# Attention, then two expert layers: the V products and row sums of a pair of heads gathered into three stretches

## The chip, the cores and the metric

The kernel runs on one core of a Trainium2 chip. The metric is the device time of one execution in microseconds (us). The kernel before has three timed runs; one further execution was recorded by the hardware profiler, and every row shown here is from that one.

## The reference, cut to what matters

```python
def _attn_ref(q, k, v, f):            # batch 4, heads 8, S = 576, D = 64
    scores = scale * np.matmul(q, k.transpose(0, 1, 3, 2))
    cum = np.cumsum(np.log(np.clip(f, 0.0001, 1.0)), axis=-1)
    scores = np.where(causal, -1e9, scores + cum[:, :, :, None] - cum[:, :, None, :])
    attn = np.exp(scores - np.max(scores, axis=-1, keepdims=True))
    attn = attn / (np.sum(attn, axis=-1, keepdims=True) + 1e-09)
    return np.matmul(attn, v)
...
x = attn_out as 2304 tokens x 512
h = x @ w_in; x = (h * sigmoid(h)) @ w_out      # 512 -> 2048 -> 512
x = soft mixture of 8 experts over x (phi, w1, w2)
```

The weights `w_in` and `w_out` arrive as 64-bit numbers, two 32-bit words each, and the kernel turns them into single precision itself. The change is to the attention alone; the two layers behind it stay as they are.

## The kernel before, in words

**Pairs and half steps.** The 32 heads are worked in 16 pairs. The loop runs over half steps `i`; `p, h = divmod(i, 2)` gives the pair and the half. `att_step(i, cv)` reads its half of the string `ORDER` (the two halves are divided by `|`) and issues one small piece of work for each word. The engines' queues are in program order, so this string is the order in which TensorE, VectorE (DVE), ScalarE (ACT), GpSimd (POOL) and the DMA queue on SyncE (SP) see their work. Several stages are in flight at a time: in the two half steps of pair `p` the kernel computes the scores of pair `p`, the products with V and the row sums of pair `p-1`, the row maxima one and a half pairs ahead, and it prepares Q and K of pair `p+2` and loads pair `p+3`.

**The words.**
- `s0` to `s5` (`s_piece`): two score matmuls into one of three banks, then the exponential on ACT (L232), then on POOL the causal select (L234).
- `m0` to `m5` (`max_piece`): one matmul (L178) into one of three other banks and a masked maximum on DVE (L184). The last block has two column ranges: `m4` reduces the first into `Mx` (L181), `m5` the second into a column of `Mt`.
- `f0`, `f1` (`max_fin_a`, `max_fin_b`): the maximum of those two columns (L197); then a transpose on TensorE, a copy to `mr` on DVE (L206), and a DMA of the maxima into row 127 of `QA`, which the score matmuls read.
- `v0` to `v3` (`av`): seven pieces of the products with V a pair (L269). The operands are plain single precision, so each piece is four matmuls (two heads, two passes); a head fills 64 columns of the array. `r` (`row_sums`): 44 matmuls of 32 columns (L252), a copy `RS` on ACT (L255), a DMA `sg<-RS`.
- `n` (`norm_b`): reciprocals of the sums on DVE (L284, L285), a DMA `R<-sg` to memory, and four DMAs `RB<-R` that read it back spread over the partitions. `b` (`norm_c`): three DVE multiplications by `RB` (L305).
- `q0`, `q1` (`split_hi`): two ACT copies each that round Q (`QA`, `QB`) and K (`KA`, `KB`). `z0`, `z1` (`split_lo`): their remainders on POOL (L154, L156).
- `l0` (`load`): one DMA of 1152 KB with Q and K of a pair, into two buffers in turn. `w`: V of a pair. `p` (`spread`): two small rows of `KA`.
- `c`: a phase of the conversion of a raw weight block. Eight blocks are converted in the attention, beginning at the half steps `CONV_AT`, in four phases each; at the end of the last, `release()` lets `pump()` issue the next raw load of 512 KB.

The 24 further raw blocks are converted in the first part of the dense layer, which starts when the attention's buffers are given back.

Of the kernel before, what the change touches and what calls it, by code (L numbers as in the profile page):

```python
# [9 lines left out]
F32 = mybir.dt.float32  # L10
F32R = mybir.dt.float32r
# [6 lines left out]
ORDER = "v0 m0 q0 v1 v2 m1 m2 s0 s1 f0 m3 z0 p s2 a3 s3 m4 r s4 l0 s5 c m5 z1 f1 | q1 v0 v1 s0 l1 f0 f1 s1 s2 z0 b n v2 m0 m1 v3 m2 w s3 m3 s4 z1 m4 s5 m5 a3 c"  # L18
CONV_AT = (2, 6, 10, 14, 18, 22, 28, 29)
# [14 lines left out]
def tile_attention_moe_softmoe(ctx: ExitStack, tc: tile.TileContext, qk, vr, f, wcat, phi, w1, w2, out):  # L34
# [35 lines left out]
    fc = ld.tile([NH, 2, S], F32, name="fc", tag="qk", bufs=2)  # L70
# [50 lines left out]
    def load(p):  # L121
# [7 lines left out]
        t = ld.tile([128, 2, 2, S], F32, name="qk", tag="qk", bufs=2)  # L129
        staged[p] = t[:, 0], t[:, 1]  # L130
        nc.sync.dma_start(out=t, in_=src)
# [6 lines left out]
    def split_hi(p, which):  # L138
        src = staged[p][which]
        nm, keep_in = (("QB", QB), ("KB", KB))[which]  # L140
        t = keep_in[p] = att.tile([128, 2, S], F32R, name=nm, tag=nm, bufs=3)
        if which:
            nc.scalar.activation(KA[p % 3][0:64], src[0:64], AF.Copy)
            nc.scalar.activation(t[64:128], src[64:128], AF.Copy)
        else:
            nc.scalar.activation(QA[p % 3][0:64, :, 64:640], src[0:64], AF.Copy)
            nc.scalar.activation(t, src, AF.Copy)  # L147
# [21 lines left out]
    def max_piece(i, j):  # L169
# [12 lines left out]
        else:  # L182
            junk = att.tile([128, 448], BF16, name="junk", tag="junk", bufs=2)
            nc.vector.tensor_tensor_reduce(out=junk[:, 0:w], in0=t[:, 0:w], in1=mask[:, 448 - w:448], scale=1.0,  # L184
                                           scalar=-3e38, op0=ALU.add, op1=ALU.max,
# [4 lines left out]
    MAXED, FIN = set(), []  # L190

    def max_fin_a():
        if not FIN and fins and 2 * fins[0][0] + fins[0][1] + fins[0][2] - 1 in MAXED:
            FIN.append(fins.pop(0))
            p, h0, n = FIN[0]
            last = Mt[p][:, h0:h0 + n, 4:5]
            nc.vector.tensor_tensor(last, last, Mx[p][:, h0:h0 + n], ALU.max)  # L197

    def max_fin_b():
        if not FIN:  # L200
            return
        p, h0, n = FIN.pop()
# [35 lines left out]
    SUMS, READY, done = set(), set(), {"r": 0, "n": 0, "b": 0}  # L238
# [43 lines left out]
    def norm_b(p):  # L282
# [4 lines left out]
        nc.sync.dma_start(out=r, in_=sg)  # L287
        if p < NPAIR - 1:
# [18 lines left out]
    def att_step(i, cv):  # L307
# [7 lines left out]
        def cvt(n, ph):  # L315
            if ph == 0:
                conv_b(n)
                conv_c(n)
            elif ph == 1:
                conv_d(n, 0)  # L320
                conv_d(n, 1)
            elif ph == 2:
# [7 lines left out]
        for op in ORDER.split("|")[h].split():  # L330
# [12 lines left out]
            elif k == "q" and 0 <= p + 2 < NPAIR:  # L343
                split_hi(p + 2, h)
# [12 lines left out]
            elif k == "c":  # L357
                for n, ph in cv:
                    cvt(n, ph)
# [691 lines left out]
```

## Time and profile before

| | us |
|---|---|
| median of three runs | 590.6 |
| lowest, highest | 589.3, 594.24 |
| profiled execution, its own time | 591.06 |
| its span in the trace | 589.2 |
| TensorE busy | 542.8 (92%) |
| ACT, DVE, POOL busy | 327.5, 320.7, 214.0 |

The span runs from the first to the last instruction; the execution's own time is 1.9 us longer. Busy TensorE is counted from modelled ends of pipelined matmuls, so a stretch can be full and still have slack in it. Attention fills roughly the first 215 us.

### The profile page before, as it was taken

The page shows a single profiled execution, that of the slowest core. Times are in us where ns is not written, and L with a number is a line of the kernel's source. Part 1 is how long each engine was busy: PE and PEld are TensorE (multiplying, and loading weights), DVE is VectorE, ACT ScalarE, POOL GpSimd, SP SyncE. Part 2 cuts the span into 40 slices and gives each one's busy share as a digit, 9 for nine tenths or more (in the row PEclk, how much of TensorE's full clock was granted, in tenths as well). Part 3 has the DMA queues.
Part 4 walks back from the last instruction along what each step waited for, and adds up shares of the span by engine and source line. Part 5 has one row for each costly group of instructions (what it writes and reads, how often), then busy time and mean ns, then how long its engine had stood idle before and what let it go on. Part 6 is the DMA issues. An engine that isn't in the chain of part 4 may idle for free.

```text
span 589.2 us, 11255 instructions
## 1 busy us (share of the span) xinstructions
PE 542.8 (92%) x4151; PEld 377.2 (64%) x4151; DVE 320.7 (54%) x889; ACT 327.5 (56%) x686; POOL 214.0 (36%) x294
## 2 busy tenths in 40 slices
PE   3589999999999999899999999999989999969993
PEld 2466666666666777677777777667666667624542
DVE  7557667677575569999989422422522431321113
ACT  5588878887877576467646544433433423322022
POOL 6378777787767421656465200000000000002000
PEclk9999999999999999999999999999999999988997
DMA  5655555646552267702431501121332228499978
GB/s 208 195 180 161 173 179 165 216 132 194 172 171 74 64 181 300 267 36 72 143 108 72 215 0 37 44 101 36 108 144 71 95 73 305 163 350 348 348 243 256
DMA packets 49528, 94.32 MB, mean 160 GB/s; under 512 B 7330, under 2 KB 34754, under 8 KB 47554
## 3 DMA queue, kind: packets, MB, share of 16 engines
q1 hardware_dynamic: 49474, 93.61, 48.3%
q8 instruction: 32, 0.52, 0.4%
q14 instruction: 22, 0.18, 0.1%
HBM read 83.64 MB, written 9.13 MB: 157 GB/s over the span
## 4 chain that ended last, share of the span: by engine, by line
PE 75%; DVE 9%; ACT 6%; DMA 5%; issue 3%; POOL 1%; SPq 0%; ACTq 0%; DVEq 0%; POOLq 0%
PE h L539 9%; PE h L541 9%; PE h L540 9%; PE av L269 7%; PE gtp L571 6%; PE mx L178 5%; PE rs L252 5%; PE st L227 5%; PE st L229 3%; PE lp L580 3%; PE pp L689 3%; DMA qk<-in_qk_dram 3%; PE so L818 3%; PE h L752 2%; DVE wt L445 2%
## 5 line engine op out<-in xcount | busy, mean ns | idle before, releaser
L539 PE MATMUL h<-w,xh 128*128 128x512 f32 x288 | 117.0, 406 | 2.6 <-DVE gt L561 2.5
L541 PE MATMUL h<-w,xh 128*128 128x512 f32 x288 | 113.6, 394 | 0.0
L540 PE MATMUL h<-w,xl 128*128 128x512 f32 x288 | 113.4, 394 | 0.0
L561 DVE SCALAR_TENSOR_TENSOR gt<-gt,h 128x512 f32<-128x512 f32 (+1 forms) x73 | 48.5, 675 | 104.8 <-ACT gt L554 104.7
L554 ACT ACTIVATE gt<-h 128x512 f32<-128x512 f32 (+1 forms) x73 | 42.8, 590 | 88.8 <-PE h L541 83.1
L184 DVE CUSTOM_DVE_ANT_0 junk<-mx,mask 128x64 bf16<-128x64 f32 (+4 forms) x160 | 65.9, 428 | 35.0 <-PE mx L178 32.2
L178 PE MATMUL mx<-KA,QA 127*128 127x256 f32 (+2 forms) x192 | 64.0, 378 | 15.7 <-POOL QB L156 9.3
L234 POOL TENSOR_SCALAR_AFFINE_SELECT E<-E 128x128 f32<-128x128 f32 (+1 forms) x160 | 52.0, 338 | 54.2 <-ACT E L232 53.0
L727 POOL MEMSET SM<- 128x512 f32 x2 | 1.1, 526 | 192.6 <-ACT gt L554 190.2
L232 ACT ACTIVATE E<-st 128x256 f32<-128x256 f32 (+2 forms) x192 | 63.4, 389 | 10.7 <-PE st L229 9.4
L227 PE MATMUL st<-QA,KA 128*128 128x256 f32 (+1 forms) x192 | 60.9, 328 | 4.3 <-ACT E L232 4.0
L539 PEld LDWEIGHTS h<-w,xh 128*128 128x128 f32 x288 | 54.1, 188 | 16.4 <-DVE gt L561 4.4
L541 PEld LDWEIGHTS h<-w,xh 128*128 128x128 f32 x288 | 54.1, 188 | 12.8
L540 PEld LDWEIGHTS h<-w,xl 128*128 128x128 f32 x288 | 54.2, 188 | 11.2
L269 PE MATMUL av<-E,VF 128*64 128x320 f32 (+4 forms) x448 | 60.0, 373 | 0.0
L178 PEld LDWEIGHTS mx<-KA,QA 127*128 127x128 f32 x192 | 36.1, 202 | 35.5 <-POOL QB L156 9.3
L229 PE MATMUL st<-QB,KB 128*128 128x256 f32 (+1 forms) x192 | 54.6, 299 | 0.0
L572 ACT ACTIVATE gr<-gtp 128x512 f32<-128x512 f32 x72 | 38.9, 593 | 18.4 <-PE gtp L571 18.4
L227 PEld LDWEIGHTS st<-QA,KA 128*128 128x128 f32 x192 | 35.4, 185 | 18.9 <-ACT E L232 8.8
L156 POOL TENSOR_TENSOR QB<-qk,QB 64x576 fp32r<-64x576 f32 x30 | 42.9, 1431 | 7.3 <-ACT QB L147 5.0
L571 PE MATMUL gtp<-ident,gt 128*128 128x128 f32 x288 | 40.2, 282 | 3.9 <-ACT gr L572 2.3
L571 PEld LDWEIGHTS gtp<-ident,gt 128*128 128x128 f32 x288 | 30.7, 141 | 17.1 <-issue 6.7
(145 smaller groups left out, 853.4 us busy)
## 6 DMA issues: line engine op xcount, KB each, us to landing
unit<-in_w_dram SPq DMA_DIRECT2D x64, 512.0 KB
qk<-in_qk_dram SPq DMA_DIRECT2D x15, 1152.0 KB
raw<-in_w_dram SPq DMA_DIRECT2D x32, 512.0 KB
VF<-in_v_dram SPq DMA_DIRECT2D x16, 320.0 KB
RB<-R SPq DMA_DIRECT2D x64, 72.0 KB
WO<-wt SPq DMA_DIRECT2D x8, 512.0 KB
unit<-WO SPq DMA_DIRECT2D x8, 512.0 KB
out_dram<-ob SPq DMA_DIRECT2D x16, 256.0 KB
```

The costliest lines, as they stand in the source:

```text
L178: nc.tensor.matmul(t[:, 0:n], lhsT=qa[0:127, h, 128 * blk:128 * blk + 128], rhs=ka[0:127, h, k0:k0 + n], start=True, stop=True)
L184: nc.vector.tensor_tensor_reduce(out=junk[:, 0:w], in0=t[:, 0:w], in1=mask[:, 448 - w:448], scale=1.0, scalar=-3e38, op0=ALU.add, op1=ALU.max,
L227: nc.tensor.matmul(t[0:m, 0:n], lhsT=ka[:, h, k0:k0 + m], rhs=qa[:, h, 64 + q0:64 + q1], start=True, stop=False)
L229: nc.tensor.matmul(t[0:m, 0:n], lhsT=kb_[:, h, k0:k0 + m], rhs=qb[:, h, q0:q1], start=False, stop=True)
L232: nc.scalar.activation(e[0:m, c0:c0 + n - skip], t[0:m, skip:n], AF.Exp, scale=0.125)
L234: nc.gpsimd.affine_select(out=e[0:m, 0:m], in_=e[0:m, 0:m], pattern=[[1, m]], compare_op=ALU.is_ge, fill=0.0, base=0, channel_multiplier=-1)
L269: nc.tensor.matmul(AVP[p][x][64 * h:64 * h + 64, o0:o0 + n], lhsT=VF[p % 2][0:k, kb, h], rhs=E[2 * p + h][kb][0:k, c:c + n], start=kb == 0 ...
L539: nc.tensor.matmul(o, lhsT=xh[:, d, tok], rhs=w[:, 0], start=(d == 0), stop=False)
L540: nc.tensor.matmul(o, lhsT=xl[:, d, tok], rhs=w[:, 0], start=False, stop=False)
L541: nc.tensor.matmul(o, lhsT=xh[:, d, tok], rhs=w[:, 1], start=False, stop=(d == 3))
L561: nc.vector.scalar_tensor_tensor(g, g, 1.0, h[:, n * j:n * j + n], op0=ALU.add, op1=ALU.mult)
L571: nc.tensor.transpose(tp[:, j, 128 * t:128 * t + 128], g[:, t, 128 * u:128 * u + 128], ident)
```

## The change

`ORDER` is written anew. The products with V of a pair stand in two places, `v0 v1 v2 v3` at the start of the first half step (pieces 0 to 3) and `v1 v2 v3` in the middle of the second (pieces 4 to 6); with the row sums `r` that makes three stretches. Score pieces and maximum pieces alternate. The remaining words follow:

- `max_fin_a` and L197 go. The maximum of `m5` begins from `Mx` (a pointer operand in place of the constant), and one `f` does the rest, behind the second stretch of V products.
- `split_hi` is four words of one ACT copy each: `q1` (KA), `q0` (QA), `q3` (KB), `q2` (QB). `split_lo` names matrix and head; the remainder of Q's second head is made half a step later (`z01`).
- Q and K of a pair are two DMAs of 576 KB into buffers of their own, `l1` (K) and `l0` (Q).
- `norm_b` ends with `R<-sg`; the four `RB<-R` become a word of their own, `x` (`norm_x`), in the next half step. `n` moves to the end of the second half step.
- Conversion phases 0 to 4 in place of 0 to 3; `CONV_AT` ends in 26, 28. The raw loads of the attention are no longer issued from the end of a conversion, but by a new word `g`, which stands just ahead of `n`.
- `spread` runs one pair earlier, at the end of the second half step.

```diff
-ORDER = "v0 m0 q0 v1 v2 m1 m2 s0 s1 f0 m3 z0 p s2 a3 s3 m4 r s4 l0 s5 c m5 z1 f1 | q1 v0 v1 s0 l1 f0 f1 s1 s2 z0 b n v2 m0 m1 v3 m2 w s3 m3 s4 z1 m4 s5 m5 a3 c"
-CONV_AT = (2, 6, 10, 14, 18, 22, 28, 29)
+ORDER = "q1 v0 v1 v2 v3 s0 m0 s1 m1 a3 s2 m2 x z01 l1 s3 m3 q0 c r l0 s4 m4 s5 m5 | s0 m0 s1 m1 s2 m2 q3 v1 v2 v3 b f q2 s3 z10 m3 s4 m4 z11 s5 m5 w p z00 f g n c"
+CONV_AT = (2, 6, 10, 14, 18, 22, 26, 28)
...
-        t = ld.tile([128, 2, 2, S], F32, name="qk", tag="qk", bufs=2)
-        staged[p] = t[:, 0], t[:, 1]
-        nc.sync.dma_start(out=t, in_=src)
+        for c in cs:
+            t = ld.tile([128, 2, S], F32, name="qk"[c], tag="qk"[c], bufs=2)
+            staged.setdefault(p, [None, None])[c] = t
+            nc.sync.dma_start(out=t, in_=src[:, c])
...
+    def split_hi(p, j):
+        src = staged[p][j % 2]
+        if j == 0:
+            nc.scalar.activation(QA[p % 3][0:64, :, 64:640], src[0:64], AF.Copy)
+        elif j == 1:
             nc.scalar.activation(KA[p % 3][0:64], src[0:64], AF.Copy)
+        elif j == 2:
+            QB[p] = att.tile([128, 2, S], F32R, name="QB", tag="QB", bufs=3)
+            nc.scalar.activation(QB[p], src, AF.Copy)
+        else:
+            KB[p] = att.tile([128, 2, S], F32R, name="KB", tag="KB", bufs=3)
+            nc.scalar.activation(KB[p][64:128], src[64:128], AF.Copy)
...
-                                           scalar=-3e38, op0=ALU.add, op1=ALU.max,
+                                           scalar=Mx[p][:, h] if j == 5 else -3e38, op0=ALU.add, op1=ALU.max,
...
-            last = Mt[p][:, h0:h0 + n, 4:5]
-            nc.vector.tensor_tensor(last, last, Mx[p][:, h0:h0 + n], ALU.max)
...
         nc.sync.dma_start(out=r, in_=sg)
+        RT[p] = r
+
+    def norm_x(p):
+        r = RT[p]
...
             if ph == 0:
                 conv_b(n)
+            elif ph == 1:
                 conv_c(n)
-            elif ph == 1:
+            elif ph == 2:
...
+            elif k == "x" and done["x"] < done["n"]:
+                norm_x(done["x"])
+                done["x"] += 1
...
+            elif k == "g":
+                pump()
...
-        release(*(x for x in (sl,) if x))
+        if sl:
+            release(sl)
...
-            cv = [(n, i - b) for n, b in enumerate(CONV_AT) if 0 <= i - b < 4]
+            cv = [(n, i - b) for n, b in enumerate(CONV_AT) if 0 <= i - b < 5]
```

## Rows read from the trace of the kernel before

**Rows 1.** Busy time by stretch: length, PE, PEld, DVE, ACT, POOL, clock, DMA.
```profile
109.43:121.35 11.92, 11.71 (x110) 8.00 (x110) 8.43 (x32) 9.66 (x21) 9.09 (x15) 1.00 0.66 196
121.35:133.19 11.84, 11.71 (x110) 8.00 (x109) 8.12 (x31) 10.34 (x22) 9.56 (x16) 1.00 0.50 156
...
215.00:300.00 85.00, 82.21 (x407) 64.36 (x404) 82.79 (x144) 51.21 (x99) 41.79 (x29) 1.00 0.44 160
```

**Rows 2.** TensorE in order of time (start, length): row sums, first and thirteenth.
```profile
37.93 1.31 PE L252 MATMUL rs<-E,ones 128*32 128x288 f32 x30
...
183.28 1.78 PE L252 MATMUL rs<-E,ones 128*32 128x288 f32 x44
```

**Rows 3.** Chain of waits, one piece of it.
```profile
100.53 5.45 DMA qk<-in_qk_dram
```

**Rows 4.** TensorE in order of time, around the V products of one pair.
```profile
111.88 1.30 PE L269 MATMUL av<-E,VF 128*64 128x320 f32 x8
113.11 0.39 PE L227 MATMUL st<-QA,KA 128*128 128x256 f32 x1
113.33 0.28 PE L229 MATMUL st<-QB,KB 128*128 128x256 f32 x1
113.45 0.27 PE L204 MATMUL mtp<-ident,Mt 128*10 128x128 f32 x1
...
116.72 0.38 PE L178 MATMUL mx<-KA,QA 127*128 127x288 f32 x1
117.03 0.65 PE L269 MATMUL av<-E,VF 128*64 128x256 f32 x4
117.61 0.39 PE L178 MATMUL mx<-KA,QA 127*128 127x256 f32 x1
117.93 0.98 PE L269 MATMUL av<-E,VF 128*64 128x128 f32 x8
118.84 0.53 PE L178 MATMUL mx<-KA,QA 127*128 127x256 f32 x2
```

**Rows 5.** TensorE where the maxima have ended and V pieces stand together.
```profile
208.63 0.81 PE L269 MATMUL av<-E,VF 128*64 128x192 f32 x8
209.37 0.41 PE L227 MATMUL st<-QA,KA 128*128 128x320 f32 x1
...
210.19 1.41 PE L269 MATMUL av<-E,VF 128*64 128x256 f32 x12
211.53 1.78 PE L252 MATMUL rs<-E,ones 128*32 128x288 f32 x44
```

**Rows 6.** DMA issues on SyncE in order of time: start, length.
```profile
98.38 0.53 SPq L136 DMA_DIRECT2D VF<-in_v_dram  x1
99.02 0.27 SPq L164 DMA_DIRECT2D KA<-cumd  x1
...
114.07 0.80 SPq L207 DMA_DIRECT2D QA<-mr  x1
115.23 0.35 SPq L287 DMA_DIRECT2D R<-sg  x1
118.28 0.66 SPq L295 DMA_DIRECT2D RB<-R  x1
...
200.60 0.34 SPq L287 DMA_DIRECT2D R<-sg  x1
202.11 0.66 SPq L295 DMA_DIRECT2D RB<-R  x1
...
207.06 0.45 SPq L417 DMA_DIRECT2D raw<-in_w_dram  x1
...
211.43 0.62 SPq L295 DMA_DIRECT2D RB<-R  x1
```

**Rows 7.** VectorE in order of time: copy of the maxima, multiplications by RB.
```profile
113.76 0.28 DVE L206 CAST mr<-mtp 10x128 fp32r<-10x128 f32 x1 [1.11 <-PE mtp L204]
...
207.35 0.90 DVE L305 TENSOR_TENSOR x<-UB,RB 128x256 f32<-128x256 f32 x3 [2.92 <-DMA RB<-R]
```

More of the change, by code (lines that the diff above doesn't have):

```diff
@@ L67, in tile_attention_moe_softmoe @@
     warm = keep.tile([1, 1], F32, name="warm")
-    fc = ld.tile([NH, 2, S], F32, name="fc", tag="qk", bufs=2)
+    fc = ld.tile([NH, 2, S], F32, name="fc", tag="q", bufs=2)
     ft, c8 = fc[:, 0], fc[:, 1]
@@ L119, in tile_attention_moe_softmoe, with load @@
     QB, KB = {}, {}
-    def load(p):
+    def load(p, cs=(0, 1)):
         b, hp = divmod(p, NP)
@@ L188, in max_piece, with max_fin @@
             MAXED.add(i)
[L190 to L195, printed above, removed]
-            last = Mt[p][:, h0:h0 + n, 4:5]
-            nc.vector.tensor_tensor(last, last, Mx[p][:, h0:h0 + n], ALU.max)
-    def max_fin_b():
-        if not FIN:
+    MAXED = set()
+    def max_fin():
+        if not (fins and 2 * fins[0][0] + fins[0][1] + fins[0][2] - 1 in MAXED):
             return
-        p, h0, n = FIN.pop()
+        p, h0, n = fins.pop(0)
         tp = bank(RING_T, [5 * n, 128], "mtp")
@@ L237, in tile_attention_moe_softmoe @@
     AVP, U, RT = {}, {}, {}
-    SUMS, READY, done = set(), set(), {"r": 0, "n": 0, "b": 0}
+    SUMS, READY, done = set(), set(), {"r": 0, "n": 0, "x": 0, "b": 0}
     CUT = 144
@@ L317, in cvt @@
                 conv_b(n)
+            elif ph == 1:
                 conv_c(n)
-            elif ph == 1:
+            elif ph == 2:
                 conv_d(n, 0)
                 conv_d(n, 1)
-            elif ph == 2:
+            elif ph == 3:
                 conv_d(n, 2)
@@ L343, in att_step @@
             elif k == "q" and 0 <= p + 2 < NPAIR:
-                split_hi(p + 2, h)
-            elif k == "z" and 0 <= p + 2 < NPAIR:
-                split_lo(p + 2, h, int(j))
+                split_hi(p + 2, int(j))
+            elif k == "z" and 0 <= (i + 3) // 2 < NPAIR:
+                split_lo((i + 3) // 2, int(j[0]), int(j[1]))
             elif k == "f":
-                (max_fin_b if j == "1" else max_fin_a)()
+                max_fin()
             elif k == "n" and done["n"] < min(done["r"], NPAIR - 1):
@@ L351, in att_step @@
                 done["n"] += 1
-            elif k == "b" and done["b"] < done["n"] and done["b"] in READY:
+            elif k == "b" and done["b"] < done["x"] and done["b"] in READY:
                 norm_c(done["b"])
                 done["b"] += 1
-            elif k == "p" and h == 0 and 0 < p + 2 < NPAIR:
-                spread(p + 2)
+            elif k == "p" and 0 < p + 3 < NPAIR:
+                spread(p + 3)
+            elif k == "x" and done["x"] < done["n"]:
+                norm_x(done["x"])
+                done["x"] += 1
             elif k == "c":
@@ L359, in att_step @@
                     cvt(n, ph)
+            elif k == "g":
+                pump()
             elif k == "w" and 0 <= p + 1 < NPAIR:
                 load_v(p + 1)
-            elif k == "l" and h == 0 and 3 <= p + 3 < NPAIR:
-                load(p + 3)
+            elif k == "l" and 3 <= p + 3 < NPAIR:
+                load(p + 3, (int(j),))
     FREE, units = [], []
@@ L912, in tile_attention_moe_softmoe @@
             norm_b(p)
+        for p in range(done["x"], NPAIR - 1):
+            norm_x(p)
         for p in range(done["b"], NPAIR - 1):
@@ L992, in tile_attention_moe_softmoe @@
                 norm_b(NPAIR - 1)
+                norm_x(NPAIR - 1)
             if k == 3:
```

8 lines of the change are left out of this document (removed).

## Prediction

> **What bounds the kernel now.** I read the busy time by stretch first. Behind the attention DVE is busy for 82.79 of 85 us in the third row [rows 1], with conversions that cannot begin before the attention gives its buffers back. So whatever the attention's end moves, the end of the kernel moves too, one to one, and only the attention is costed here. Its pace is read off the row sums, of which there is one stretch a pair: from the first to the thirteenth it is (183.28 - 37.93) / 12 = 12.11 us a pair [rows 2]; two ordinary pairs take 11.92 and 11.84, with TensorE busy for 11.71 of each [rows 1]. That looks like TensorE and nothing else, but the chain of waits tells of a second bound of the same length: it runs through the load of Q and K, 5.45 us [rows 3]. This load stands in SP's queue behind the copy `sg<-RS`, so behind this pair's row sums, and the two copies of the next pair's `q0` wait for it, with the exponentials and the next row sums behind them: a loop that closes once a pair. A faster TensorE alone would run into it.
>
> The TensorE rows show why a full engine still has something to give. The granted clock is 1.00 there [rows 1], and between full-width matmuls the next start comes after about 2.4 columns a nanosecond: 0.12 us for 256 columns (113.33 to 113.45 [rows 4]). Around a stretch of V products it does not. The matmul ahead, 288 columns, takes 0.31 (116.72 to 117.03); the first one behind, 256 columns, takes 0.22 in place of 0.12 (113.11 to 113.33); one between two stretches takes 0.32 (117.61 to 117.93). The stretch has a cost of its own too: its columns pass at 1.2 a nanosecond, twice, and on top come 0.15 to 0.16: a lone piece of 256 columns takes 0.58 (2 x 0.213 + 0.15), pieces 3 and 4 together 1.23 (4 x 0.267 + 0.16) [rows 4].
>
> **Part 1, three stretches for six.** Before, a pair has five stretches of V products: 0.58, 0.91, 1.23 [rows 4], and the last two pieces 0.74 as they stand together in one row [rows 5]; 3.46 in all. After: pieces 0 to 2 together take 1.34 (210.19 to 211.53 [rows 5]), against 0.58 + 0.91 = 1.49 apart, so merging takes off 0.15; piece 3 adds 2 x 0.267 = 0.53: 1.87. Pieces 4 to 6: 0.53 + 0.74 = 1.27. Sum 3.14, gain 0.32. Pieces 5 and 6 differ in the rows of the array that they fill (128 and 64); that they stand apart before costs no less than the 0.74, so this can only understate the gain. Three first-matmuls-behind fewer: 3 x 0.10 = 0.30. Entries: 0.18 ahead of two of the five (0.31 less 0.13 for 288 columns), about 0.1 ahead of the others; 0.66 becomes 0.18 + 0.10, gain 0.38. Together 1.0 us a pair, and TensorE's own pace 11.71 - 1.0 = 10.7, or 10.6, since some of the 11.71 is itself the tail of a wait.
>
> The row shows that 64-column and full-width work do not follow each other freely, at about 0.35 a stretch. The Trainium skill ("TensorEngine Tiling (Array Packing)", Tiling Modes) has the rule: a change of tiling mode drains the engine. By it the 128-to-64-row step inside the second stretch stays, as the 0.74 has it; without it the second stretch would be 1.12, and the sum 2 us better over the attention.
>
> **Part 2, two loads for one.** The same bytes, one more issue of about 0.45 on SP (as the raw load's issue [rows 6]); behind it waits `sg<-RS`, which waits for the row sums anyway. K is now needed first and is issued ahead of `sg<-RS`; Q is needed only at `q0`, half a pair later than before. The loop of [rows 3] opens by several us: I take it as gone. With it go the two pairs of some 13 us that the mean of 12.11 has over the ordinary 11.9.
>
> **Part 3, the round trip of the sums: the new loop.** Before, `n` issued `R` early in a second half step, the four `RB` DMAs followed, and `b` used them a whole pair later. Now `n` is at the end of the second half step, `x` follows in SP's queue, and `b` stands in the middle of the next second half step, on DVE ahead of the copy `mr` and of the maxima `m3` to `m5`. The matmul of `m5` needs the bank that `mr` empties (three banks in turn), and the next pair's first V stretch is queued behind it. So: `mr`, then `R`, then `RB`, then `b`, then the next `mr` is a loop that closes once a pair. Its length: from `mr` to the issue of `R` it was 1.47 (113.76 [rows 7] to 115.23 [rows 6]), with `QA<-mr` in between; now V (0.64 from issue to issue, 98.38 to 99.02) and the rows of KA (0.27) are issued there also, and DVE needs the three maxima first: I take 2.1. From `R` to the first `RB`: 1.51 with nothing in flight (200.60 to 202.11), 3.05 behind a load of 1152 KB (115.23 to 118.28) [rows 6]; now V's 320 KB is ahead, so 2.3, in the middle. First `RB` to the multiplications: 5.24 (202.11 [rows 6] to 207.35 [rows 7]). Three multiplications to `mr`: 0.83 (0.90 less overlap). Sum 10.5, about TensorE's 10.6, so nothing is left over.
>
> In five of these twelve pairs the word `g` puts a raw load of 512 KB just ahead of `R`. The nearest row: a raw load issued at 207.06, the first `RB` at 211.43, 4.37 later [rows 6]. With its issue, 0.45, the loop becomes 2.1 + 4.8 + 5.2 + 0.4 = 12.5 (the first term without the part that the raw load now covers would be 12.0 at the least). A pair of 12.5 is not made good by the next, whose own loop is 10.5. Before, the raw loads went out early in a second half step, where nothing of that pair waited for them.
>
> **Part 4, at nothing.** L197 goes, two columns wide and off TensorE's path. The pointer operand of `m5` is in no row: 0 to 0.2 us an instruction (the small DVE operations nearby), and it lies in the loop once a pair; I take 0 and keep 2 us in the range. The four ACT copies are the same; `q1` now lies under the first V stretch, `q0` under the row sums, `q3` under the second stretch, where ACT has no scores to work on. Without that cover each would hold up a score bank for 1.1 us. POOL's remainders are needed a pair later and keep that slack. Five conversion phases have the same instructions; DVE's in the first half step now lie under the row sums. `spread` makes SP wait for the pair's last score matmul, with raw load and `R` behind it; the 0.27 is counted. Start-up: the same loads with two more issues, -1 to +1, taken as 0.
>
> **The sum**, against the profiled execution's 591.06. Twelve intervals before: 145.35. After: 7 x 10.6 + 5 x 12.5 = 136.7, less 0.8 for the time that `m5` can wait in the first late pair: 135.9, a gain of 9.4. The thirteenth interval gains 1.0, the first pair and the last two one stretch each, 0.3 to 0.4: together 1.1. 591.06 - 11.5 = 579.5; I say **579**. The median before lies 0.5 under the profiled run, within its spread.
>
> **Rivals.** *The loop has slack* (if `R` lands within 1.5 us, and the raw load passes it or is covered): TensorE's 10.6 holds in all twelve: 127.2, gain 18.1 + 2.1: 571. For it: 1.51 is seen, and V is small. Against it: `R` has waited behind whatever was queued in every other row.
>
> *ACT becomes the bound.* It is busy for 10.0 a pair (mean of 9.66 and 10.34 [rows 1]); at 10.6 it would be 94% full, and in an in-order queue that meets banks of three, not all of its idle time of 1.9 can go. If 1.6 of it stays, the pace is 11.6: 145.4 - 139.2 = 6.2 and 1 at the ends: 584. The Trainium skill ("Perfetto Trace Analysis", Identifying the Most-Contended Engine) speaks for it: matmul busy time is no measure of how near TensorE is to its limit, LDWEIGHTS busy is, while for ACT occupancy is. By that TensorE is at 8.0 of 11.92 and ACT at 84% the engine to relieve, and this change relieves it of nothing.
>
> *Slower: the sums' round trip runs behind the half loads.* If K or Q is still in flight when `R` is issued, because `sg<-RS` holds Q back, `R` waits for up to half of 5.45 more. The loop is then 13.2, and 15.2 with a raw load: 7 x 13.2 + 5 x 15.2 = 168.4, 23 us more, 612. It decides from a mean loop of 12.11, which is reached when `R` to `RB` takes 0.8 us more than my mean.
>
> *The change does not do what it says:* stretches merge but the cost sits in the weights of each piece, and the new order gives it back in waits; 587 to 592.
>
> **How the numbers follow.** A run of this kernel can tell about 1% from no change, 5.9 us. Chances: the forecast 0.43 (574 to 584), the loop with slack 0.25 (567 to 574), ACT 0.13 (581 to 588), no gain 0.11, slower by the round trip 0.08. Faster by over 1% (under 585): nearly all of the first two and over half of the third, 0.75. Slower by over 1%: 0.08. Within 1%: 0.17. The range leaves out the upper tail of the last two and a little below: 567 to 590.
>
> **What would show it.** The V products in two stretches a pair of about 1.87 and 1.27; row sums 10.6 apart, and some 12 apart where a raw load lies ahead of `R`; no ACT wait for Q and K in the ordinary pairs; DVE idle ahead of its multiplications by `RB`, and TensorE at the last maximum of a pair waiting for DVE. Wrong if ACT shows no idle time and TensorE waits for exponentials, if `RB` has landed well before its use, or if the layer behind the attention does not move with it.

## The result and the profile after

The changed kernel takes 597.0 us (median of four runs), the kernel before 590.9 on the same chip: a ratio of 1.013, 95% interval 1.008 to 1.017. It is slower by 1.3% where I had forecast 2% faster. The profiled execution took 599.4 us, with a span of 597.7; it is 2.4 us slower than the median, and the rows below are read from it.

First the row sums on TensorE (start, length), which answer to [rows 2], and the first matmul of the layer behind the attention.

```profile
40.50 1.31 PE L248 MATMUL rs<-E,ones 128*32 128x288 f32 x29
...
189.27 1.78 PE L248 MATMUL rs<-E,ones 128*32 128x288 f32 x44
...
223.12 0.50 PE L546 MATMUL h<-w,xh 128*128 128x512 f32 x1
```

The first row sums come 2.6 us later than before, the twelve intervals take 148.8 us instead of 145.4 (a mean of 12.40 instead of 12.11), and from the thirteenth row sums to the first `h` matmul it is 33.9 instead of 31.8 (before, that matmul stood at 215.05). Together 8.1 us, and the whole span is longer by 8.5: what the attention loses, the end loses.

The busy time of two neighbouring pairs, from row sums to row sums, in the columns of [rows 1]; the second one waits for an `RB` whose `R` stood behind a raw load.

```profile
88.58:99.46 10.88, 10.78 (x111) 7.99 (x110) 8.22 (x31) 10.41 (x22) 7.50 (x12) 1.00 0.68 210
99.46:112.54 13.08, 11.02 (x111) 8.05 (x110) 10.77 (x31) 9.96 (x21) 10.60 (x17) 1.00 0.52 149
```

TensorE's work for a pair did shrink, from 11.7 to 10.8 and 11.0, but in the longer pair it stands idle for 2 us. The V products are merged as forecast: in the next rows sixteen matmuls are busy for 1.95 us (1.88 up to the start of what follows, where nothing waits), and twelve take 1.27 up to that start (forecast 1.87 and 1.27; these rows answer to [rows 4, 5]).

```profile
116.45 1.34 PE L265 MATMUL av<-E,VF 128*64 128x320 f32 x12
117.72 0.28 PE L200 MATMUL mtp<-ident,Mt 128*10 128x128 f32 x1
...
119.11 1.95 PE L265 MATMUL av<-E,VF 128*64 128x256 f32 x16
```

Where the idle time ends is in the waits of TensorE and of VectorE over these twelve pairs (total, times, longest).

```profile
PE mx L181 <- DVE mr L202: 10.0, 7, 3.8
PE st L223 <- DMA QA<-mr: 6.6, 7, 1.4
```
```profile
DVE x L305 <- DMA RB<-R: 13.9, 7, 3.3
```

In the kernel before TensorE waits for neither. The two waits follow from each other, as the rows of one pair with a raw load show (VectorE's `mr`, SP's issues, VectorE again, TensorE; these answer to [rows 6, 7]).

```profile
94.10 0.28 DVE L202 CAST mr<-mtp 10x128 fp32r<-10x128 f32 x1
```
```profile
96.16 0.84 SPq L423 DMA_DIRECT2D raw<-in_w_dram  x1
97.09 0.37 SPq L283 DMA_DIRECT2D R<-sg  x1
101.01 0.66 SPq L295 DMA_DIRECT2D RB<-R  x1
...
105.05 0.41 SPq L132 DMA_DIRECT2D q<-in_qk_dram  x1
106.92 0.79 SPq L203 DMA_DIRECT2D QA<-mr  x1
```
```profile
105.81 0.90 DVE L305 TENSOR_TENSOR x<-UB,RB 128x256 f32<-128x256 f32 x3 [1.51 <-DMA RB<-R]
106.62 0.27 DVE L202 CAST mr<-mtp 10x128 fp32r<-10x128 f32 x1
```
```profile
106.95 0.40 PE L181 MATMUL mx<-KA,QA 127*128 127x288 f32 x1 [0.74 <-DVE mr L202]
107.28 1.95 PE L265 MATMUL av<-E,VF 128*64 128x256 f32 x16
110.55 0.35 PE L223 MATMUL st<-QA,KA 128*128 128x256 f32 x1 [1.33 <-DMA QA<-mr]
```

From `mr` to `mr` this is the loop of the prediction's third part, 12.52 us. `R` waits 3.9 us to land behind the raw load; the multiplications wait for `RB`; `mr` stands behind them on VectorE; the last maximum waits for `mr`; and `QA<-mr`, issued late and 1.9 us behind Q's half load, lets the next pair's scores wait once more. The chain of waits from 40.5 to 189.3 us passes through `R` and `RB` in seven of the twelve pairs, the five with a raw load and two more, and these are the seven in which VectorE waits for `RB`. One of the two without a raw load, in the chain:

```profile
133.29 2.74 DMA R<-sg
...
139.29 3.24 DMA RB<-R
...
142.65 0.90 DVE x L305 x3
```

The waits cost more than their length. In the kernel before, the granted clock is 1.00 from 30 to 224 us. Here it falls three times in the attention, each time shortly behind a wait of TensorE or at its end: it is 0.61 from 36 to 40 us (a wait of 3.76), 0.74 from 185 to 189 (3.84) and 0.75 from 209 to 213 (1.84). The same work takes longer there: 3.47 us instead of 1.99 for the scores and maxima ahead of the first row sums, 3.62 instead of 1.95 for sixteen V matmuls, and for 44 matmuls of row sums 3.24 instead of 1.78:

```profile
211.14 3.24 PE L248 MATMUL rs<-E,ones 128*32 128x288 f32 x44
```

Together that is 4.6 of the 8.1 us.

### The profile page after: what moved, and what is told of

It reads as the page before. It is cut to its first block, busy times and chain, and to the rows that moved or that the text cites. A ratio compares the mean times of both kernels' runs of the same rounds, so it can differ in the third digit from the quotient of the medians.

```text
span 597.7 us, 11293 instructions
## 1 busy us (share of the span) xinstructions
PE 531.6 (89%) x4151; PEld 379.4 (63%) x4151; DVE 330.7 (55%) x872; ACT 332.5 (56%) x686; POOL 213.2 (36%) x294
## 4 chain that ended last, share of the span: by engine, by line
PE 57%; DMA 15%; DVE 12%; ACT 5%; SPq 4%; issue 3%; POOL 1%; DVEq 0%; ACTq 0%; POOLq 0%
PE h L546 9%; PE h L547 9%; PE h L548 9%; DMA R<-sg 6%; PE gtp L578 6%; DMA RB<-R 5%; PE lp L587 3%; PE pp L696 3%; PE so L825 3%; SPq L295 2%; PE h L759 2%; DVE x L305 2%; DMA QA<-mr 2%; PE st L223 2%; PE mx L181 2%
## 5 line engine op out<-in xcount | busy, mean ns | idle before, releaser
L228 ACT ACTIVATE E<-st 128x256 f32<-128x256 f32 (+2 forms) x192 | 67.0, 389 | 31.6 <-PE st L225 24.4
L230 POOL TENSOR_SCALAR_AFFINE_SELECT E<-E 128x128 f32<-128x128 f32 (+1 forms) x160 | 50.0, 331 | 58.1 <-ACT E L228 55.8
L187 DVE CUSTOM_DVE_ANT_0 junk<-mx,mask 128x64 bf16<-128x64 f32 (+3 forms) x128 | 53.4, 422 | 29.7 <-PE mx L181 29.2
L548 PEld LDWEIGHTS h<-w,xh 128*128 128x128 f32 x288 | 54.5, 189 | 12.9
L181 PEld LDWEIGHTS mx<-KA,QA 127*128 127x128 f32 x192 | 38.3, 204 | 30.7 <-issue 14.3
L225 PE MATMUL st<-QB,KB 128*128 128x256 f32 (+1 forms) x192 | 57.3, 301 | 0.0
L265 PE MATMUL av<-E,VF 128*64 128x320 f32 (+4 forms) x448 | 54.8, 376 | 0.0
L159 POOL TENSOR_TENSOR QB<-q,QB 64x576 fp32r<-64x576 f32 x30 | 43.7, 1458 | 6.4 <-ACT QB L147 4.1
```

Source lines behind the costliest of these rows:

```text
L181: nc.tensor.matmul(t[:, 0:n], lhsT=qa[0:127, h, 128 * blk:128 * blk + 128], rhs=ka[0:127, h, k0:k0 + n], start=True, stop=True)
L225: nc.tensor.matmul(t[0:m, 0:n], lhsT=kb_[:, h, k0:k0 + m], rhs=qb[:, h, q0:q1], start=False, stop=True)
L228: nc.scalar.activation(e[0:m, c0:c0 + n - skip], t[0:m, skip:n], AF.Exp, scale=0.125)
L230: nc.gpsimd.affine_select(out=e[0:m, 0:m], in_=e[0:m, 0:m], pattern=[[1, m]], compare_op=ALU.is_ge, fill=0.0, base=0, channel_multiplier=-1)
L265: nc.tensor.matmul(AVP[p][x][64 * h:64 * h + 64, o0:o0 + n], lhsT=VF[p % 2][0:k, kb, h], rhs=E[2 * p + h][kb][0:k, c:c + n], start=kb == 0 ...
L548: nc.tensor.matmul(o, lhsT=xh[:, d, tok], rhs=w[:, 1], start=False, stop=(d == 3))
```

## Experiments

In all of them the edits are to words of `ORDER`, if nothing else is said; the diffs show the words around the edit. Times are medians; the kernel before ran beside them each time at 589.2 to 590.6, and ratios are to it, with a 95% interval. "Interval" is the mean of the twelve intervals of row sums, "R to RB" the mean time from issue to issue in the same pairs.

**Raw loads behind the sums.**

```diff
-w p z00 f g n c
+w p z00 f n g c
```

> The changed kernel with the raw loads issued behind R in place of just ahead of it. Round-trip theory (the loop R to RB to the multiplications to the copy of the maxima sets the pace, and a raw load ahead of R lengthens it): the intervals that hold a raw load, 13.1 to 14.2 us, fall by 1.5 to 2.5 each, R is followed by RB after some 2.5 us in place of 4 to 4.5, and the kernel comes to about 587. Queue theory (the copies QA<-mr wait behind the loads of Q and K whatever stands ahead of R): those intervals stay, since RB, K and Q are in flight as before; 595 to 597.

Measured: 590.1 us, ratio 1.000 (0.997 to 1.004). R to RB fell from 2.91 to 2.25, the interval from 12.40 to 11.61. That takes back the whole loss, and none of the forecast gain: TensorE's 10.8 is not reached. Of the 12 us between the two profiled runs some 3 are the stretches at a lower clock near 185 and 211 us, which this run does not have.

**Multiplications late**, and both together.

```diff
-v1 v2 v3 b f q2
+v1 v2 v3 f q2
...
-s5 m5 w p z00 f g n c
+s5 m5 b w p z00 f g n c
```

> The changed kernel with the three multiplications by RB moved from ahead of the copy of the maxima to behind the last maximum of the half step; raw loads stay ahead of R. Round-trip theory: the copy mr and the last three maxima no longer wait for RB, so TensorE waits neither at the last maximum nor, through QA<-mr, at the first score; intervals of 10.6 to 11 without a raw load, up to 12 with one; about 580. Queue theory: the copy QA<-mr still lands 3.5 us after its issue behind Q's load, and the first scores of a pair still wait for it by 1 us or so; 590 or more.

> Both at once: the multiplications behind the last maximum and the raw loads behind R. Round-trip theory: the pace is TensorE's own, 10.6 to 10.8 in every interval, and the kernel comes to 572 to 576. Queue theory: little better than the multiplications late alone, about 590.

Measured: 605.7 us, ratio 1.026 (1.022 to 1.029), and 608.1, ratio 1.031 (1.027 to 1.034). A miss: with `b` out of the way of `mr` the kernel got slower. Two things show in the trace of the first one. `QA<-mr` now goes out as little as 0.7 us behind Q's half load, and TensorE waits for it 13.1 us between 40 and 180 us, up to 3.2 at a time, where the changed kernel waits 6.6: this is what the queue theory named. And VectorE's work takes longer, as the rows of VectorE and GpSimd at the end of one second half step show.

```profile
109.77 2.19 DVE L305 TENSOR_TENSOR x<-UB,RB 128x256 f32<-128x256 f32 x3
111.89 1.39 DVE L280 TENSOR_SCALAR sg<-sg 96x12 f32<-96x12 f32 x1
```
```profile
109.78 1.67 POOL L157 TENSOR_TENSOR KB<-k,KA 64x576 fp32r<-64x576 f32 x1
...
111.86 1.39 POOL L157 TENSOR_TENSOR KB<-k,KA 64x576 fp32r<-64x576 f32 x1
```

The three multiplications take 2.19 us instead of 0.90, and the first operation on the sums, 12 columns wide, 1.39 instead of 0.16. (It adds 1e-9 to them, L280; the expectations call it the sums' copy, and so does the text from here on.) The multiplications begin with one remainder of `split_lo` on GpSimd and end 0.5 us behind it; the copy begins 0.03 us into the next one and ends 0.03 behind it. I had not reckoned with this at all. How the loss divides between the two was not measured.

**The kernel before, with V pieces merged** (one load of Q and K, sums as they were).

```diff
-v0 m0 q0 v1 v2 m1 m2
+v0 v1 v2 m0 q0 m1 m2
...
-q1 v0 v1 s0 l1 f0 f1 s1 s2 z0 b n v2 m0 m1 v3 m2 w
+q1 v0 v1 v2 v3 s0 l1 f0 f1 s1 s2 z0 b n m0 m1 m2 w
```

> The kernel before with one edit: pieces 0 to 2 of the V products stand together at the start of a pair and pieces 3 to 6 together at the start of its second half, so three stretches for six; loads, sums, maxima and conversions as before. If the boundaries of the stretches are what TensorE's pace is made of and nothing else binds, a pair gains 0.9 to 1.0 us, 14 us in all: 577. If the load of Q and K behind the row sums closes a loop of its own of 11.9, as I read it from the chain of waits, a pair keeps 11.7 to 11.9: 587 to 591.

Measured: 593.8 us, ratio 1.003 (0.999 to 1.006), interval 12.26. With TensorE's work reduced (it is busy for 65.3 of the 72 us from 90 to 162, before for 70.9) nothing comes of it. But it is not the load that takes the gain: ACT waits for Q once, for 0.8 us (7.1 us in eight waits in the kernel before, 40 to 180 us), and the load lies on the chain of waits in two of the twelve pairs. TensorE waits twice a pair for exponentials, which stand on ACT behind its copies of Q and K:

```profile
PE st L227 <- ACT E L232: 12.3, 23, 1.6
```

So the second bound that merging alone meets is ACT's copies. The changed kernel has them under the V products and the row sums, and there TensorE's matmuls wait for ACT 0.9 us in twelve pairs.

**Maxima first.**

```diff
-q3 v1 v2 v3 b f q2
+q3 f v1 v2 v3 b q2
```

> The changed kernel with the maxima's step (transposition, copy to mr, the DMA into Q's spare rows) ahead of the V products and the multiplications, so that the copy to mr no longer stands behind the wait for RB on VectorE and the DMA into Q is issued some 2.5 to 3 us earlier in the half step; the raw weights stay ahead of the sums. If what closes the pair is the multiplications holding mr and the DMA into Q behind them: the first scores and m5 no longer wait, intervals fall by the 1.3 to 2.5 us a pair of waits for mr and for the DMA into Q seen in the pairs with a raw load, about 1.0 a pair as a mean, 582 to 587 us (ratio 0.985 to 0.995). If the loss is VectorE's work slowed down beside GpSimd's remainders, nothing of this is touched: 594 to 598 us (ratio 1.006 to 1.013).

Measured: 590.1 us, ratio 1.001 (0.998 to 1.004), interval 11.89. The wait for `mr` is gone; R to RB is still 2.77, and `QA<-mr` now goes out 0.46 us behind Q's half load and keeps the scores waiting, up to 2.1 us.

```profile
103.26 0.41 SPq L132 DMA_DIRECT2D q<-in_qk_dram  x1
103.72 0.79 SPq L203 DMA_DIRECT2D QA<-mr  x1
```
```profile
109.39 0.36 PE L223 MATMUL st<-QA,KA 128*128 128x256 f32 x1 [2.10 <-DMA QA<-mr]
```

**Late multiplications with the remainders moved.**

```diff
-v3 s0 m0 s1 m1 a3 s2 m2 x z01
+v3 s0 m0 z11 s1 m1 a3 s2 m2 z00 x z01
...
-s4 m4 z11 s5 m5 b w p z00 f n g c
+s4 m4 s5 m5 b w p f n g c
```

> The kernel with late multiplications and raw loads behind the sums (608 us), with the two GpSimd remainders of the end of the second half step, z11 and z00, moved into the first half step that follows, away from the multiplications, the copies of the sums and the conversions. Theory of a shared way into SBUF: VectorE's 64-wide multiplications go back from 1.02 to about 0.2 us and the sums' copies from 0.5 to 0.16, some 2 us a pair off the chain on VectorE: 580 to 590 us. Rival (the lengthening has nothing to do with GpSimd, or the late multiplications lose for another reason, their wait for RB and the maxima's step behind them): 603 to 610 us, as without the move.

Measured: 599.8 us, ratio 1.017 (1.010 to 1.025). Inconclusive: `z10`, left where it was, now ran beside the multiplications (their last piece still took 1.4 us in 7 of 11 pairs).

**Sums early, maxima first**, and the same with fewer raw loads at the start.

```diff
-v3 s0 m0 s1 m1 a3 s2 m2 x z01 l1
+v3 l1 s0 m0 s1 m1 a3 s2 m2 z01
...
-q3 v1 v2 v3 b f q2
+q3 f v1 v2 v3 b n x q2
...
-w p z00 f g n c
+w p z00 f g c
```

The second of the two kernels also has, in the loop over half steps:

```diff
             if i == 1:
-                mo["cap"] = 3
+                mo["cap"] = 1
+                pump()
+            if i == 3:
+                mo["cap"] = 3
                 pump()
```

> The changed kernel with three moves: the step of the maxima ahead of the V products; the sums copied and sent to DRAM, and the broadcast RB issued, in the middle of the second half step, as in the kernel before, instead of at its end and in the next first half step; K's half load ahead of the first scores. The round trip through DRAM then has a whole second half and first half step, and the multiplications wait for nothing. If the wait for RB and what stands behind it are the loss: intervals of 10.8 to 11.4, 573 to 582 us (ratio 0.97 to 0.985). If VectorE beside GpSimd's remainders is the main loss, the sums' copies leave the place beside the remainders only in part: 585 to 592. If TensorE's clock or the start-up make up the loss: about 590 and over.

> The same as the run with early sums, and one raw load instead of three ahead of the second pair's DMA into Q at the start (the cap of 3 comes two half steps later). If the 2.6 us by which the first row sums of the changed kernel come later are those loads ahead of the small DMA on the queues: 2 to 3 us faster than the run without it, with first row sums at 38 us instead of 40.5. If the first row sums are late because of the load of Q that waits for GpSimd: within 1 us of it.

Measured: 595.9 us, ratio 1.009 (1.006 to 1.013), and 596.3, ratio 1.011 (1.008 to 1.015). Misses. In the first, SP waits for `R` to land at the word `x`, and V's load and the rows of KA stand behind it; TensorE's waits name them:

```profile
PE mx L181 <- DMA KA<-cumd: 10.8, 8, 2.1
```

The second has its first row sums at 36.3 instead of 39.4, as expected, but gives 2.2 of the 3 us back in the pairs (interval 12.44 instead of 12.26), and the medians are the same; I did not follow up why.

**Q's load behind the maxima**, then **the sums ahead of the loads** as well.

```diff
-q0 c r l0 s4 m4 s5 m5 |
+q0 c r s4 m4 s5 m5 |
...
-q3 v1 v2 v3 b f q2
+q3 f l0 v1 v2 v3 b q2
...
-s5 m5 w p z00 f g n c
+s5 m5 n w p z00 f g c
```

(The first of the two has only the first two edits.)

> The run with the maxima first (590.1 us), and Q's half load moved from the end of the first half step to just behind the maxima's DMA into Q, so that the small DMA no longer shares the queues with a load issued 0.5 us ahead of it. If what that run still lost is that DMA (it landed 4 to 5.7 us after its issue, and the first scores waited for it 7.8 us in 6 pairs between 40 and 180 us): it lands after 2 to 3 us, the waits go, mean interval of twelve from 11.89 to 11.0 to 11.2, and 577 to 582 us (ratio 0.978 to 0.987). If VectorE beside GpSimd's remainders holds the pair anyway: 587 to 591.

> The same with the sums' copy and their DMA R ahead of V's load and of the raw weights at the end of the second half step. Every small transfer of the pair then goes out ahead of the large one that was next to it: R to RB 1.4 to 2 us in all pairs instead of 1.5 to 3.4. By the theory that the pair's time is that of small transfers behind large ones: 1 to 4 us less than the run with Q's load behind the maxima alone. If that loop has slack by then: the same within 1 us. Slower by 2 us or more if VectorE's wait for the sums holds up the second half step's maxima.

Measured: 590.1 us, ratio 0.999 (0.996 to 1.002), and 580.7, ratio 0.987 (0.984 to 0.990). The first is a miss: R to RB rose to 3.21, with Q's load now closer ahead of `R`. The second is faster than the kernel before, with R to RB at 1.87 and an interval of 11.49. TensorE's waits for `mr` and `QA<-mr` between 42 and 180 us are down from 12.7 us in the changed kernel to 0.3; what is left are 4.6 us for the maxima in `Mt`. Its small transfers each stand ahead of a large one:

```profile
109.06 0.79 SPq L203 DMA_DIRECT2D QA<-mr  x1
109.95 0.41 SPq L132 DMA_DIRECT2D q<-in_qk_dram  x1
112.56 0.34 SPq L283 DMA_DIRECT2D R<-sg  x1
112.99 0.38 SPq L137 DMA_DIRECT2D VF<-in_v_dram  x1
...
113.83 1.06 SPq L423 DMA_DIRECT2D raw<-in_w_dram  x1
```

**K's remainders on VectorE**, in the changed kernel and on top of the last one.

```diff
-        eng = nc.vector if p < 2 and which == 1 else nc.gpsimd
+        eng = nc.vector if which == 1 else nc.gpsimd
```

> The changed kernel with K's two remainders a pair (z10, z11) on VectorE instead of GpSimd, and nothing else. It adds some 2 x 0.75 us of VectorE a pair (an estimate from the multiplications' 0.42 us for 256 columns and 0.21 for 64) and takes away the two GpSimd operations at the end of the second half step behind which VectorE's operations end late. Theory of the shared way into SBUF: the sums' first copy is back at 0.16 us, the conversions at 0.43 to 0.7; if this is the main part of the loss, 585 to 592 us. If the loss is the small transfers behind the half loads: 594 to 600 us, though the operations are short again.

> The run with the sums ahead of the loads, with K's remainders on VectorE as well. If the two mechanisms add up: 1 to 4 us below it, 573 to 578 us. If VectorE's added 1.5 us a pair costs as much as the late ends did: the same within 2 us, or slower.

Measured: 600.3 us, ratio 1.017 (1.011 to 1.023), and 586.2, ratio 0.994 (0.989 to 0.998); against 597.0 and 580.7 without it. The added work on VectorE costs more than it saves, and neither tells more, for not all operations became short: the sums' copy fell to 0.25 us in most pairs, but Q's remainders stayed on GpSimd and met the conversions instead (L451 at 1.3 to 1.8 us in every conversion up to 190 us).

**Maxima late again**, and **Q's load back**, both from the kernel of 580.7.

```diff
-q3 f l0 v1 v2 v3 b q2
+q3 v1 v2 v3 b f l0 q2
```
```diff
-q0 c r s4 m4 s5 m5 |
+q0 c r l0 s4 m4 s5 m5 |
...
-q3 f l0 v1 v2 v3 b q2
+q3 f v1 v2 v3 b q2
```

> The run with the sums ahead of the loads (580.7 us), with the maxima's step back behind the V products and the multiplications, Q's load still behind it. If the copy to mr behind VectorE's wait for RB was a loss of its own: 2 to 8 us slower (583 to 589), with m5 or the first scores waiting for mr again. If the order of the transfers alone was the loss, the wait for RB is short by now: within 1.5 us of 580.7.

> The run with the sums ahead of the loads, with Q's half load back at the end of the first half step, some 0.5 us ahead of the DMA of the maxima. If that small DMA behind Q's load is the larger loss: 586 to 590 us, with 4 to 5.5 us from issue to landing and the first scores waiting for it. If the order of R, V's load and the raw weights is the larger: 580 to 584.

Measured: 589.5 us, ratio 1.001 (0.998 to 1.004), and 583.5, ratio 0.989 (0.984 to 0.994). The first has TensorE waiting for `mr` again, 8.6 us in 7 of the pairs up to 180 us; but as `l0` follows `f`, Q's load moved too, closer ahead of `R` (R to RB 2.85), so it is two changes, and the 9 us are not all the maxima's. Some 3 of them are the clock: it is 0.57 from 153 to 161 us, behind a wait of 3.6 us. The second has an interval of 11.44, as good as with the load behind: between pairs the place of Q's load does not matter once the maxima go first and the sums go out ahead of V's load (with the maxima first alone, TensorE still waited 7.8 us for `QA<-mr`). What it costs is the start: first row sums at 40.5 instead of 35.5, a part of it again at a lower clock (0.66 from 34 to 44 us). The rows of the changed kernel show that start (GpSimd; SP; TensorE).

```profile
27.54 1.41 POOL L159 TENSOR_TENSOR QB<-q,QB 64x576 fp32r<-64x576 f32 x1
```
```profile
28.97 0.35 SPq L132 DMA_DIRECT2D q<-in_qk_dram  x1
29.37 1.38 SPq L423 DMA_DIRECT2D raw<-in_w_dram  x3
30.85 0.77 SPq L203 DMA_DIRECT2D QA<-mr  x1
```
```profile
37.03 0.55 PE L223 MATMUL st<-QA,KA 128*128 128x256 f32 x1 [3.76 <-DMA QA<-mr]
```

Q's load needs the buffer that a remainder on GpSimd frees at 28.95; SP stands there, and the small `QA<-mr` behind it and three raw loads lands 6 us after its issue.

**No remainders on GpSimd**, from the kernel of 586.2.

```diff
-        else:
-            eng.tensor_tensor(t[64:128, h], src[64:128], t[64:128, h], ALU.subtract)
```

> The run with all three moves (586 us; K's remainders on VectorE), without Q's two remainders a pair, so that GpSimd has no two-operand work of the splitting left (Q's low part stays the copy; this part of the computation is changed). VectorE's own work is that of the run with all three. Theory that VectorE's operations on SBUF start only after GpSimd's remainder has ended: all conversions at 0.43 to 0.7 us, the sums' copy at 0.16, the waits for Mt and the longer intervals of the pairs with a conversion (12.3 to 12.6) go: 574 to 579 us. If those waits are due to the conversions' own work: within 2 us of 586.

Measured: 576.3 us, ratio 0.979 (0.974 to 0.983), interval 10.94; TensorE's waits for VectorE fall from 5.2 us to 0.4. This kernel leaves out Q's remainders, a part of the computation, so it only measures. Groups of VectorE instructions from 42 to 180 us (count, sum in us, mean ns), first in the changed kernel, then here (the kernel is two lines shorter, so L451 is L449 here):

```profile
L451 DVE SCALAR_TENSOR_TENSOR wt<-raw,wt 128x512 int32<-128x512 int32 x6 | 8.4, 1398 | 0.0
L457 DVE TENSOR_SCALAR raw<-wt 128x512 int32<-128x512 int32 x5 | 6.5, 1291 | 0.2
L280 DVE TENSOR_SCALAR sg<-sg 96x12 f32<-96x12 f32 x11 | 5.2, 472 | 0.0
```
```profile
L449 DVE SCALAR_TENSOR_TENSOR wt<-raw,wt 128x512 int32<-128x512 int32 x7 | 4.8, 692 | 0.0
...
L455 DVE TENSOR_SCALAR raw<-wt 128x512 int32<-128x512 int32 x6 | 2.7, 452 | 0.2
L278 DVE TENSOR_SCALAR sg<-sg 96x12 f32<-96x12 f32 x13 | 2.7, 208 | 0.0
```

With no such work on GpSimd every one of them is short. The 10 us against 586.2 bound the price from above: without the remainders GpSimd also comes to its masks earlier.

**Conversions behind the maxima**, from the kernel of 580.7.

```diff
-q3 f l0 v1 v2 v3 b q2
+q3 f c l0 v1 v2 v3 b q2
...
-n w p z00 f g c
+n w p z00 f g
```

> The run with the sums ahead of the loads (580.7 us), with the conversions' step of the second half step moved from its end, where GpSimd runs its remainders, to just behind the copy to mr, ahead of the V products, where GpSimd has only the masks. Theory of late ends behind the remainders: the moved conversions back at 0.43 to 0.7 us, TensorE's waits for Mt (4.6 us in 4 in the part up to 180 us) mostly gone, the pairs with a conversion at 11.2 to 11.6: 575 to 579 us. If the conversions then hold up the multiplications and m3 instead: 580 to 584.

Measured: 579.5 us, ratio 0.983 (0.980 to 0.987), interval 11.23: the lowest time here of a kernel that computes everything, though only 1.2 us under 580.7, which the intervals do not separate. TensorE's waits for `Mt`, 4.6 us before, do not appear; of the two moved operations the second takes 0.43 as a mean against 1.16, the first, 0.95 against 0.98, still meets a remainder or a mask in most pairs.

**The sums' copy and the other conversion step apart**, from the kernel of 579.5.

```diff
-s3 z10 m3 s4 m4 z11 s5 m5 n w p
+s3 z10 m3 s4 m4 s5 m5 n z11 w p
```

(The second one also has `q0 c r s4 m4 s5 m5 |` as `q0 r s4 m4 s5 m5 c |`.)

> The run with the conversions behind the maxima (579.5 us), with K's second remainder z11 behind the sums' copy and R instead of ahead of them, so that the copy no longer stands behind a remainder on GpSimd (it took 0.9 to 1.4 us instead of 0.16 in 9 of 15 pairs). Theory of late ends: the copy back at 0.16 to 0.27 us, R out some 0.8 us earlier, 0 to 0.5 us a pair: 573 to 579 us. If GpSimd's remainders then come too late for the scores: 582 and over.

> The same with the conversions' step of the first half step moved to its end, behind Q's remainder on GpSimd. Theory of late ends: the first conversion step (1.4 to 1.7 us in 4 of 7, 0.42 to 0.46 in the others) at 0.42 to 0.5, 0 to 3 us below the run without it. If it then holds up the second half step's maxima: 1 to 4 us above.

Measured: 583.2 us, ratio 0.989 (0.985 to 0.993), and 586.4, ratio 0.995 (0.992 to 0.997). Misses: GpSimd is so far behind that the copy meets `z10`, not `z11` (1.0 us as a mean in 8 of 15 pairs), so the move helped nothing; in the second the copy took 1.0 to 1.4 in 11 of the first 14 pairs, and the conversions' operation L451 1.2 as a mean of six. A word's place in `ORDER` does not say when GpSimd gets to it.

## Why the prediction was wrong

**What bounds the kernel** held in one half: the attention's loss went to the end nearly one to one (8.1 and 8.5 us). The other half held in part: ACT does wait for Q in the kernel before (7.1 us in eight waits), but the bound that merging alone met was another, exponentials behind ACT's copies. The forecast's remark that each copy needs the cover of a long stretch on TensorE was the one that counted.

**Part 1** held: 1.88 + 1.27 us for the two stretches, and the shortest intervals of the changed kernel are 10.84 to 10.88, 0.2 above my 10.6.

**Part 2** held in that no long wait for K or Q is left. But I priced the second load as one more issue. It cost more at its neighbours: `QA<-mr` behind Q's half load, and the start, which comes 2.6 us later. There SP stands at Q's load until GpSimd has freed its buffer, and 1.5 of the 2.6 us are the lower clock behind that wait.

**Part 3 is the step that failed: the loop was the right one, but its price was not, and the wait for `QA<-mr` was put at nothing.** The loop `mr`, `R`, `RB`, multiplications, `mr`, worked out for the twelve pairs from the starts in the trace (means in us, forecast in brackets):

| | 5 pairs with a raw load | 2 more that wait for `RB` | 5 others |
|---|---|---|---|
| `mr` to `R` | 2.79 (2.1) | 2.34 (2.1) | 2.90 |
| `R` to first `RB` | 3.89 (4.8, with the raw issue, which here lies in the row above) | 2.86 (2.3) | 1.95 |
| first `RB` to multiplications | 5.35 (5.2) | 6.52 (5.24) | 5.61 |
| multiplications to `mr` | 1.09 (0.4) | 0.82 (0.83) | 1.17 |
| sum | 13.11 (12.5) | 12.53 (10.5) | 11.63 (10.6, TensorE) |

The twelve sums add up to 148.8 whatever sets the pace, for `mr` comes once a pair; the forecast had 135.9. That is 12.9 of the 19.9 us by which the profiled run missed. In the first seven pairs VectorE waits for `RB`, so the loop paces seven pairs and not five. In the other five `RB` has landed 0.1 to 1.0 us before the multiplications begin, and something else ended last.

- *The five with a raw load* took 3.1 us more, and the 0.8 that I took off did not come off. Most of it is a slip of my sum: it has 0.4 for the multiplications to `mr`, which I had put at 0.83 before. With 0.83 it would have been 12.97. The row that I used for `R` behind a raw load (207.06 to 211.43) begins at the raw load's issue, so I counted that issue twice, and `R` stands 2.3 us behind it there. That 4.8 came out near the truth is luck: from the raw load's issue to `RB` it is 4.85 in the rows shown above.
- *The two more* took 3.9 us more than the 10.6 each that TensorE was to set: `R` to `RB` was longer by 0.55, and `RB`'s way back took 6.5 us where I had one row of 5.24.
- *The five others* took 5.1 us more. TensorE waits there 2.7 us for `QA<-mr` and 0.9 for ACT, and 1.7 are the lower clock. `QA<-mr` goes out late when `mr` is late, and it lands behind Q's half load; over the twelve pairs TensorE waits 6.6 us for it, and no part of the forecast has this wait.

Start and end together cost 4.7 us more where I had 2.1 less. That is the other 6.8; some 3 of it are the lower clock, and at the end the chain of waits runs through the loop again, where I had counted one gain a pair. No part of the forecast has the clock falling behind a wait either.

For `mr` to `R` the forecast was low by its own rows: 1.47, 0.64 and 0.27 make 2.38 where nothing overlaps, and I took 2.1.

The rival "slower by the round trip" named the deciding point, a mean loop of 12.11, and 12.40 lies beyond it. But hardly for its reason: `R` to `RB` was longer than I took it in two pairs only. And its 612 was too much.

**Part 4** put at nothing what GpSimd's remainders do to VectorE. "POOL's remainders are needed a pair later and keep that slack" is true of their result and says nothing of what runs beside them. The change gathers three of four remainders at the end of the second half step, beside the sums' copy and the conversions. The copy takes 0.4 to 1.3 us in six of the twelve pairs, and on the chain of the seven pairs late ends of the copy and of one multiplication add 3.1 us. One case (VectorE, then GpSimd): the copy of the sums starts 0.17 us into a remainder, ends 0.03 us behind it, and takes 1.26 instead of 0.16; the reciprocal of the same tile takes 0.22 as ever.

```profile
84.36 1.26 DVE L280 TENSOR_SCALAR sg<-sg 96x12 f32<-96x12 f32 x1
85.66 0.22 DVE L281 RECIPROCAL sg<-sg 96x12 f32<-96x12 f32 x1
```
```profile
84.19 1.40 POOL L157 TENSOR_TENSOR KB<-k,KA 64x576 fp32r<-64x576 f32 x1
```

The trace of the kernel before had shown it, in six conversions, in rows that I did not read side by side (GpSimd; VectorE: this operation takes 0.62 us where nothing delays it):

```profile
97.28 1.43 POOL L156 TENSOR_TENSOR QB<-qk,QB 64x576 fp32r<-64x576 f32 x1
```
```profile
97.99 1.27 DVE L449 SCALAR_TENSOR_TENSOR raw<-raw 128x512 int32<-128x512 int32 x1
```

The Trainium skill ("GPSIMD Engine Reference", Specifications) has the rule: GpSimd shares its SBUF interfaces with VectorE, in contention with VectorE's instructions in a 2-port perf mode or with two SBUF inputs. The trace agrees in part: the sums' copy, the conversions and the multiplications are hit, all in SBUF; the maxima, which read PSUM, are not, and neither are the reciprocals (0.22 us also where they start within a remainder, eight of them in the first run with late multiplications). The size here is up to the whole rest of GpSimd's operation, 1.4 us.

**The other rivals.** ACT did not become the bound: it is busy for 10.4 of 10.88 in a short pair, and TensorE's matmuls wait for it 0.9 us in all twelve. That the loop has slack would have been nearer the truth without the late ends: with small transfers in order and no remainders on GpSimd the interval is 10.94.

**How far the order of transfers carries.** Two moves of a single word show it best: the raw loads behind the sums took 6.9 us off (interval 12.40 to 11.61), and the sums ahead of V's load and the raw loads 9.4 (590.1 to 580.7 us, interval 12.12 to 11.49). Over seven kernels the interval goes with R to RB, though not in strict order: 2.91 and 12.40 (changed), 2.85 and 12.37 (maxima late), 3.21 and 12.12 (Q's load behind the maxima), 2.77 and 11.89 (maxima first), 2.25 and 11.61 (raw loads behind the sums), 1.87 and 11.49 (sums ahead of the loads), 1.62 and 11.44 (Q's load back). Others do not fit: 2.25 and 12.26, 2.49 and 12.44 (the two with early sums), 2.15 and 12.83 (K's remainders on VectorE). And below 1.9 it no longer decides: the interval is anywhere from 10.94 to 11.72 there. Left open is how the rest divides between the late ends on VectorE, GpSimd's general load and the lower clock (up to 0.3 us of an interval), and how much the maxima's place is worth by itself.

## What to carry to other kernels

A round trip through DRAM that closes once a period is a second clock: sum every term of it, those on busy engines with what they meet there. A sum that comes out equal to the period has no room for error: here one put at 10.5 came to 12.5 where it was the bound. In an in-order queue put each small transfer that something waits for ahead of the large one next to it. Before merging work on one engine, ask which other engine used the gaps: here ACT's copies needed them. When an operation on one engine is moved, look at what it will run beside on the other engines' way to the same memory, not only at who needs its result.

## What the hardware showed that I had not expected

VectorE's additions, conversions and multiplications in SBUF that start within a two-operand GpSimd operation end only behind it: 0.03 us behind where they take 0.16 alone, 0.29 where they take 0.43, 0.55 where they take 0.69. One of 0.16 became 1.26 us. A 5 KB transfer into `QA` that lands after 2.0 us alone takes 3.5 some 1.9 us behind a load of 576 KB, and 6.0 behind that load and three of 512 KB. And a wait of TensorE can be paid twice: behind an idle time of 3.84 us, sixteen V matmuls took 3.62 us instead of 1.95. The granted clock, 0.74 from 185 to 189 us, shows that part of them ran at the lower of its two levels, 1.2 GHz.

```profile
183.34 0.40 PE L181 MATMUL mx<-KA,QA 127*128 127x288 f32 x1 [3.84 <-DVE mr L202]
183.67 3.62 PE L265 MATMUL av<-E,VF 128*64 128x256 f32 x16
```
```profile
185.00:189.00 4.00, 4.00 (x23) 2.47 (x20) 3.02 (x9) 1.47 (x4) 1.36 (x2) 0.74 0.31 85
```
